# Second batch's keys and values moved into block diagonals, fourth batch's keys placed a step earlier

## The chip, the core and the metric

The kernel runs on one core of a Trainium2 chip. The core has a matrix engine (TensorE, "PE" in the profile, whose weight loads are shown apart as "PEld"), a vector engine (VectorE, "DVE"), an activation engine (ScalarE, "ACT"), a general engine (GpSimd, "POOL") and an engine that only issues transfers (SyncE, "SP"). TensorE writes its results into a small memory, PSUM; the others work on the larger SBUF, and DMA queues move data between it and the chip's main memory. The engines run beside each other, each through its own list of instructions in order, and wait for each other by semaphores. The metric is the device time of one launch, in microseconds (us); less is better.

## What is computed

Sliding-window attention over 8 batches, 8 heads, 576 positions and head size 64, followed by a two-layer network with a leaky ReLU. All inputs are float32.

```python
def _attn_ref(q, k, v):                       # each (8, 8, 576, 64)
    scale = 1.0 / np.sqrt(D)
    scores = scale * np.matmul(q, k.transpose(0, 1, 3, 2))
    mask = np.abs(pos[:, None] - pos[None, :]) <= 32
    scores = np.where(mask, scores, -1000000000.0)
    scores = scores - np.max(scores, axis=-1, keepdims=True)
    attn = np.exp(scores)
    attn = attn / (np.sum(attn, axis=-1, keepdims=True) + 1e-09)
    return np.matmul(attn, v)

x = attn_out.transpose(0, 2, 1, 3).reshape(4608, 512)
h = x @ w_in                                  # 512 x 2048
out = np.maximum(0.01 * h, h) @ w_out         # 2048 x 512
```

Each position sees only the 65 positions around it, so a block of 64 keys meets at most 128 queries.

## The kernel before

**Units of work.** Heads are taken in pairs, the two heads of a pair on partitions 0 to 63 and 64 to 127. A batch of 576 positions has two halves of 288, and an attention unit `i` is one batch, one half and one pair: `i = 8b + 4*half + pair` (`where`, L268), 64 units in all. For each unit there is a *score* (L271: keys times queries for five key blocks, into the PSUM tile `ps`, then the exponential on ScalarE and the multiplication by the window mask on VectorE or POOL), *sums* (L318: a matmul with block-diagonal ones adds up the probabilities of each query into the PSUM tile `s`, and VectorE takes the reciprocal), a *product* (L340: probabilities times values, into the PSUM tile `x`), and *scaled* (L372: VectorE multiplies product and reciprocal into `xT`, the network's input). From unit 12 on, a *join* (L310) on VectorE first adds the two layers of probabilities, so that the sums need one matmul and not two. The tiles `s` and `x` have one buffer each, and so has `ps`.

**The network.** A token group `g` is a half batch. `h_tile` (L416) makes one of 16 feature tiles for it in four matmuls of 288 columns, with the leaky ReLU on ScalarE; `o_tile` (L437) makes 128 rows of the output in 16 matmuls of 512 columns. These are the bulk of TensorE's work.

**Two forms of keys and values.** For the first two batches (`NATURAL = 2`) a head's keys lie in natural order, 64 partitions a head (`kTs`, made by transposes on TensorE and an eviction from PSUM, L203 and L212), and the values in `v0b[b]`, one tile for each of the two batches. Score and product then take, for each of five key blocks, one 64x64 matmul for each head: ten matmuls. From the third batch on, keys and values lie in block diagonals, `kbd[b % 2]` and `vbd[b % 2]`: 128x128 blocks with one head's 64x64 block in each of two quarters and zeros in the others. One 128x128 matmul serves both heads: five matmuls. The keys of these batches are cast on POOL (`cast_qk`, L227), transposed by DMA (`transpose_dma`, L238) and copied into the diagonal by two VectorE copies a pair (`place_keys`, L251), which also undo an interleaving. The values are loaded as float32 and cast by POOL into the diagonal (`cast_v`, L233).

**Order.** All engines' lists follow one written order. The first batch's attention is written out by hand (L513 to L636). Then come the first tiles of the network for the second half batch, between which the block diagonals are zeroed, `kbd` by VectorE and `vbd` by POOL (L640 to L644); POOL issues the second batch's value loads (L646, with the cast in the DMA); and SP issues the third batch's query and key loads (L648), which wait behind a tiny memset on POOL. After this the o tiles and h tiles run from a plan (L690 to L702). Each quarter of an o tile (four matmuls) and each h tile is a *turn*; `spend` (L710) runs, ahead of it, what the table `SECOND` (L667) names for the turn, which is all of the second batch's first half. From unit 12 on, `step` (L477) runs when it is due by the plan's own clock: join of unit `i + 1`, score of `i + 2`, sums, product and scaling of `i`, then `place_keys`, the casts and transposes, and the loads for the next batch. At which step the keys of a batch are placed is set in `transpose_dma`: for pair `p` of batch `b` in step `8(b - 1) + 4 + p`, and one step later for the fourth batch (`b == 3`, L247). The score that reads them first is `8b + p`, in step `8b + p - 2`.

`SECOND` before, in the turns that the change touches: scores 8 to 11 at turns 5, 6, 8 and 10; sums 8 at turn 7, sums 9 at turn 8 right behind score 10, product 8 at turn 9, sums 10 and product 9 at turn 11, sums 11 and product 10 at turn 13, score 12 at turn 14, product 11 and score 13 at turn 16. The third batch's casts and key transposes (`turned`) stand at turns 10, 12, 14 and 16. From `h_tile(2, 0)`, behind turn 16, the network reads what the second batch's units 8 to 11 have put into `xT`.

Of the kernel before, what the change touches and what calls it, by code (L numbers as in the profile page):

```python
# [9 lines left out]
FP32 = mybir.dt.float32  # L10
BF16 = mybir.dt.bfloat16
# [5 lines left out]
def kernel(  # L17
# [14 lines left out]
    nc = tc.nc  # L32

    B, H, S, D = q.shape
# [5 lines left out]
    NPAIR = H // 2  # L40
    NB = S // 64
    HALF = S // 2
# [20 lines left out]
    qf, kf, vf = {}, {}, {}  # L63
    RUN = S // 96

    NATURAL = 2
# [34 lines left out]
            in_=src[b, 2 * p:2 * (p + n)].rearrange("(p a) (i c) d -> (a i) p (c d)", a=2, c=ROW),  # L101
        )

    v0b = [const.tile([128, NPAIR, NB, D], BF16, name=f"v0b{i}") for i in range(NATURAL)]

    def load_v(b, p, engs=(nc.sync, nc.sync)):

        if engs[0] is nc.gpsimd:
            t = v0b[b][:, p]
        else:  # L110
            t = vf[b, p] = fload.tile([128, NB, D], FP32, name=f"vf{p}")
        for a in range(2):
            engs[a].dma_start(  # L113
                out=t[64 * a:64 * a + 64],
                in_=v[b, 2 * p + a].rearrange("(c p) d -> p c d", p=64),
            )

    load_v(0, 0, (nc.sync, nc.scalar))
# [4 lines left out]
    for p in range(1, NPAIR):  # L123
# [3 lines left out]
    ones_bd = const.tile([128, 128], BF16)  # L127


    kbd = [const.tile([128, NPAIR, NB, 128], BF16, name=f"kbd{i}") for i in range(2)]  # L130
    vbd = [const.tile([128, NPAIR, NB, 128], BF16, name=f"vbd{i}") for i in range(2)]
    zero = const.tile([128, 1], BF16)

    WIN = [
        [((0, 0, 48), (2, 48, 64), (4, 112, 32)), ((1, 16, 64), (3, 80, 64))],
        [((4, 0, 32), (6, 32, 64), (8, 96, 48)), ((5, 0, 64), (7, 64, 64))],
    ]

    def copy_to(eng, out, in_):
        if eng is nc.scalar:  # L140
            eng.activation(out=out, in_=in_, func=AF.Copy)
        else:
            eng.tensor_copy(out=out, in_=in_)

    HEADS = (slice(0, 64), slice(64, 128))
    GAP = 3 * 128
    wide = const.tile([128, GAP + 32 + 256], BF16)
    win = const.tile([128, 128], BF16)
# [1 line left out]
    for lo in (0, 64):  # L150
        w = win[lo:lo + 64]
        nc.gpsimd.affine_select(
            out=w, in_=w, compare_op=ALU.is_ge, fill=0.0,
# [3 lines left out]
            out=w, in_=w, compare_op=ALU.is_ge, fill=0.0,  # L157
# [30 lines left out]
    ps = scps.tile([128, 1024], FP32)  # L188
    P0 = 512 - HALF
# [9 lines left out]
    qT = {}  # L199

    trans, kTs = {}, {}

    def transpose_first(b, p, which):  # L203
# [3 lines left out]
        for c in range(ROW):  # L207
            for r in HEADS:
                nc.tensor.transpose(tp[r, c], src[r, p, c], ident[r, r])  # L209
        trans[b, p, which] = tp.rearrange("p c i -> p i c")  # L210

    def evict_first(b, p, which, eng):  # L212
        if which == "q":
            if b not in qT:
                qT[b] = attn.tile([128, NPAIR, S], BF16, name="qT")
            to = qT[b][:, p]
        else:
            to = kTs[b, p] = kt.tile([128, S], BF16, name="kT")
        copy_to(eng, to.rearrange("p (i c) -> p i c", c=ROW), trans.pop((b, p, which)))

    def value_first(b, p, eng):
        copy_to(eng, v0b[b][:, p], vf[b, p])

    def fill(eng):
        eng.memset(ps[:, 512:512 + HALF], 0.0)
# [12 lines left out]
    def transpose_dma(b, p):  # L238
        if b not in qT:
            qT[b] = attn.tile([128, NPAIR, S], BF16, name="qT")  # L240
        kT = kt.tile([128, S], BF16, name="kT")
        for t, src in ((qT[b][:, p], qb), (kT, kb)):
            nc.sync.dma_start_transpose(
                out=t.rearrange("p (c i) -> p c i", c=RUN),
                in_=src[:, p].rearrange("p c a d -> p (c a d)"),
            )
        landing.append((8 * (b - 1) + (5 if b == 3 else 4) + p, b, p, kT))  # L247

    unplaced, landing = [], []

    def place_keys():  # L251

        while landing and landing[0][0] <= state["done"]:
            unplaced.append(landing.pop(0)[1:])
        while unplaced:
            b, p, kT = unplaced.pop(0)
            for a in range(2):
                r = slice(64 * a, 64 * a + 64)
                to = kbd[b % 2][r, p, :, r]
                nc.vector.tensor_copy(  # L260
                    out=to.rearrange("p n (m c) -> p n c m", c=2),
                    in_=kT[r].rearrange("p (c n m) -> p n c m", c=2, n=NB),
                )
# [4 lines left out]
    def where(i):  # L268
        return i // 8, (i // 4) % 2, i % 4

    def score(i):  # L271
        b, hf, p = where(i)
        if b < NATURAL:
            by_n = ps[:, P0:P0 + 2 * HALF].rearrange("p (n t) -> p n t", n=2)
            for n_, blocks in enumerate(WIN[hf]):
                for blk, i0, n in blocks:
                    lo, hi = 2 * i0, 2 * (i0 + n)
                    for r in HEADS:
                        nc.tensor.matmul(  # L279
                            by_n[r, n_, lo:hi], kTs[b, p][r, 64 * blk:64 * blk + 64],  # L280
                            qT[b][r, p, hf * HALF + lo:hf * HALF + hi], start=True, stop=True,
                        )
        else:
            by_c = qT[b][:, p].rearrange("p (c i) -> p c i", c=2)
            for n_, blocks in enumerate(WIN[hf]):
                for blk, i0, n in blocks:
                    nc.tensor.matmul(  # L287
                        ps_v[:, n_, :, i0:i0 + n], kbd[b % 2][:, p, blk],
                        by_c[:, :, hf * EVEN + i0:hf * EVEN + i0 + n], start=True, stop=True,
                    )  # L290
        if b > 0:
            exps(i)
            masked(i, nc.vector if i in ON_DVE else nc.gpsimd)

    def exps(i):
        e = attn.tile([128, 2 * HALF], BF16, name="e")
        nc.scalar.activation(out=e, in_=ps[:, P0:P0 + 2 * HALF], func=AF.Exp, scale=scale)  # L297
        probs[i] = e

    def masked(i, eng):  # L300
        b, hf, p = where(i)
        e = probs[i]
        pr = prob[:, i % NPROB]
        allowed = mask_first[hf] if b < NATURAL else mask[hf].rearrange("p n c i -> p n (c i)")
        eng.tensor_mul(  # L305
            pr.rearrange("p n c i -> p n (c i)"), e.rearrange("p (n t) -> p n t", n=2), allowed,
        )
        probs[i] = [pr, None, None, None]
# [31 lines left out]
    def product(i):  # L340

        b, hf, p = where(i)
        pr = probs[i][0]
        x = xps.tile([128, HALF], FP32, name="x")
        x_v = x.rearrange("p (c i) -> p c i", c=2)
        flat = pr.rearrange("p n c i -> p n (c i)")
        parts = [(n_, *block) for n_ in range(2) for block in WIN[hf][n_]]
        if b < NATURAL:
            for n_, blk, i0, n in parts:
                lo, hi = 2 * i0, 2 * (i0 + n)  # L350
                for r in HEADS:
                    nc.tensor.matmul(  # L352
                        x[r, lo:hi], v0b[b][r, p, blk], flat[r, n_, lo:hi],
                        start=(blk == parts[0][1]), stop=(blk == parts[-1][1]),
                        skip_group_check=True,
                    )
        else:
            for n_, blk, i0, n in parts:
                nc.tensor.matmul(  # L359
                    x_v[:, :, i0:i0 + n], vbd[b % 2][:, p, blk, :], pr[:, n_, :, i0:i0 + n],  # L360
                    start=(blk == parts[0][1]), stop=(blk == parts[-1][1]),
                    skip_group_check=True,
                )
        probs[i][3] = x
# [275 lines left out]
    for f in range(4, FFC):  # L640
        h_tile(1, f)
        if f < 12:
            nc.vector.memset(kbd[f // 4 - 1][:, f % 4], 0.0)
            nc.gpsimd.memset(vbd[f // 4 - 1][:, f % 4], 0.0)  # L644
    make_mask(1, nc.gpsimd)
    for p in range(NPAIR):  # L646
        load_v(1, p, (G, G))
# [3 lines left out]
    def second_keys(p, eng):  # L651
        transpose_first(1, p, "k")
        evict_first(1, p, "k", eng)

    def second_queries(p, eng):
        transpose_first(1, p, "q")
        evict_first(1, p, "q", eng)
# [5 lines left out]
    def turned(p):  # L663
# [19 lines left out]
    }  # L683
# [14 lines left out]
    at, t = {}, 0.0  # L698
# [56 lines left out]
```

## Time and profile before

| | |
|---|---|
| median of 3 runs | 320.47 us (319.94 to 321.87) |
| the profiled execution's own time | 320.11 us |
| its span in the profile | 318.3 us |
| granted TensorE clock | 0.995 of full speed |
| busy: PE, DVE, POOL, ACT | 307.7, 213.8, 189.6, 168.3 us |
| matmuls | 2794 |
| moved by DMA | 46.11 MB, mean 145 GB/s |

The profile names each instruction by engine and by the line of the kernel (L279 is the second batch's score, L352 its product, L287 and L359 the same in block diagonals, L327 and L324 the sums, L388 the h matmuls, L446 the o matmuls, L209 the transposes, L260 the copies into the key diagonals). A line of a timeline gives start and length in us, then engine, line, operation, the tile written and the tile read, and how many such instructions were merged into the line; in square brackets stands how long the engine was idle before and whose end it waited for. Matmuls overlap, so the length of one is more than its share of TensorE's time, and what a group of them costs is read from its start to the start of the next group.

### The profile page before, as it was taken

Reading aid. Unit: us, or ns where it says so; the run is one execution under the profiler, and the core shown is the slowest. Engines: PE = TensorE matmul, PEld = TensorE weight load, DVE = VectorE, ACT = ScalarE, POOL = GpSimd, SP = SyncE. Lnnn points to the kernel's source line nnn. Section 1 sums busy time; section 2 is a strip of 40 time slices with the busy share of each in tenths; the row PEclk is TensorE's granted clock in tenths of the full one; section 3 lists DMA queues with packets and bytes.
Section 4 is the critical chain, followed back from the end, with each engine's and each line's share of the span. In section 5 each row is a group of like instructions: output and inputs, shape, how many; then the busy total and the mean of one; then the engine's idle time right before and its main releaser. Section 6 shows DMA issues by size and latency. Waiting matters only on the chain.

```text
span 318.3 us, 7099 instructions
## 1 busy us (share of the span) xinstructions
PE 307.7 (97%) x2794; PEld 202.6 (64%) x2794; DVE 213.8 (67%) x257; ACT 168.3 (53%) x370; POOL 189.6 (60%) x260
## 2 busy tenths in 40 slices
PE   5789999999999999999999999999999999999996
PEld 4557754575756747576765858576665857676653
DVE  3899528598665788688755997688745988565100
ACT  2655853472743827374652828465552837464531
POOL 8999954555466756686546866586637856330000
PEclk9799999999999999999999999999999999999999
DMA  8999999969997994599835997399933520000102
GB/s 131 143 186 207 206 172 235 154 118 223 251 218 187 205 227 110 77 222 207 187 76 124 235 200 168 74 236 168 214 75 106 107 70 35 32 37 3 66 21 80
DMA packets 107314, 46.11 MB, mean 145 GB/s; under 512 B 68752, under 2 KB 102800, under 8 KB 107280
## 3 DMA queue, kind: packets, MB, share of 16 engines
q1 hardware_dynamic: 91936, 37.91, 57.3%
q0 software_dynamic: 14752, 7.59, 18.0%
q8 instruction: 22, 0.36, 0.5%
q10 hardware_dynamic: 592, 0.15, 0.2%
q14 instruction: 12, 0.10, 0.2%
HBM read 36.70 MB, written 9.44 MB: 145 GB/s over the span
## 4 chain that ended last, share of the span: by engine, by line
PE 85%; DMA 6%; POOL 4%; DVE 3%; issue 1%; ACT 1%; DVEq 0%; ACTq 0%; POOLq 0%
PE mm L446 38%; PE mm L388 33%; DMA kb<-in_k_dram 6%; PE ps L287 4%; PE x L359 3%; POOL prob L305 2%; PE s L324 2%; DVE r L337 2%; PE tp L209 1%; PE ps L279 1%; POOL w_out_bf L509 1%; PE x L352 1%; DVE kbd L260 1%; PE s L327 1%; POOL w_in_bf L505 0%
## 5 line engine op out<-in xcount | busy, mean ns | idle before, releaser
L337 DVE RECIPROCAL r<-s 128x288 f32<-128x288 f32 x64 | 125.2, 1957 | 54.6 <-PE s L324 53.1
L388 PE MATMUL mm<-xT,w_in_bf 128*128 128x288 bf16 x1024 | 133.8, 286 | 0.3
L446 PE MATMUL mm<-w_out_bf,gT 128*128 128x512 bf16 (+2 forms) x592 | 131.5, 373 | 0.0
L399 ACT ACTIVATE gT<-mm 128x288 bf16<-128x288 f32 x256 | 101.7, 411 | 26.5 <-PE mm L388 10.0
L388 PEld LDWEIGHTS <-w_in_bf 128*128 128x128 bf16 x1024 | 98.2, 98 | 25.5 <-issue 0.6
L305 POOL TENSOR_TENSOR prob<-e,mask 128x576 bf16<-128x576 bf16 x48 | 61.2, 1274 | 81.3 <-issue 46.4
L446 PEld LDWEIGHTS <-gT 128*128 128x128 bf16 x592 | 55.6, 98 | 58.9
L451 ACT ACTIVATE o_sb<-mm 128x512 f32<-128x512 f32 (+2 forms) x37 | 21.7, 586 | 91.9 <-PE mm L446 91.9
L297 ACT ACTIVATE e<-ps 128x576 bf16<-128x576 f32 x64 | 41.4, 647 | 18.1 <-PE ps L287 8.0
L236 POOL CAST vbd<-vf 64x576 bf16<-64x576 f32 x48 | 33.2, 693 | 1.4
L374 DVE TENSOR_TENSOR xT<-x,r 128x288 bf16<-128x288 f32 x64 | 29.1, 454 | 6.2
L260 DVE COPY kbd<-kT 64x576 bf16<-64x576 bf16 x48 | 32.3, 672 | 0.3
L231 POOL CAST kb<-kf 96x384 bf16<-96x384 f32 x48 | 26.8, 583 | 1.6 <-DMA kf<-in_k_dram 1.6
L231 POOL CAST qb<-qf 96x384 bf16<-96x384 f32 x48 | 24.3, 535 | 5.4 <-DMA qf<-in_q_dram 5.3
L315 DVE TENSOR_TENSOR both<-prob 128x288 bf16<-128x288 bf16 x52 | 19.9, 382 | 4.4 <-POOL prob L305 3.6
L287 PEld LDWEIGHTS <-kbd 128*128 128x128 bf16 x240 | 15.3, 98 | 8.0 <-DVE kbd L260 1.6
L287 PE MATMUL ps<-qT,kbd 128*128 128x128 bf16 (+2 forms) x240 | 19.3, 211 | 0.6 <-DVE kbd L260 0.6
L359 PE MATMUL x<-prob,vbd 128*128 128x128 bf16 (+2 forms) x240 | 19.3, 211 | 0.0
L359 PEld LDWEIGHTS <-vbd 128*128 128x128 bf16 x240 | 15.5, 98 | 1.3
L305 POOL TENSOR_TENSOR prob<-e,wide 128x576 bf16<-128x576 bf16 x10 | 12.7, 1275 | 6.0 <-ACT e L297 6.0
L324 PE MATMUL s<-both,ones_bd 128*128 128x288 bf16 x52 | 14.9, 286 | 0.0
L113 POOL DMA_DIRECT2D v0b<-in_v_dram x14 | 10.4, 790 | 0.0
(47 smaller groups left out, 102.8 us busy)
## 6 DMA issues: line engine op xcount, KB each, us to landing
out_dram<-o_sb SPq DMA_DIRECT2D x35, 256.0 KB, 4.2
vf<-in_v_dram SPq DMA_DIRECT2D x49, 144.0 KB, 3.6
qf<-in_q_dram SPq DMA_DIRECT2D x24, 288.0 KB, 4.5
kf<-in_k_dram SPq DMA_DIRECT2D x24, 288.0 KB, 5.1
w_in_bf<-in_moe_w_in_dram POOLq DMA_DIRECT2D x4, 512.0 KB, 7.7
w_out_bf<-in_moe_w_out_dram POOLq DMA_DIRECT2D x4, 512.0 KB, 10.0
v0b<-in_v_dram POOLq DMA_DIRECT2D x14, 72.0 KB, 4.3
kb<-in_k_dram POOLq DMA_DIRECT2D x4, 144.0 KB, 4.4
```

Of the source, the lines that this page charges most:

```text
L231: nc.gpsimd.tensor_copy(out=dst[:, p, 3 * c:3 * c + 3], in_=by_c[c])
L236: nc.gpsimd.tensor_copy(out=vbd[b % 2][r, p, :, r], in_=vf[b, p][r])
L260: nc.vector.tensor_copy(out=to.rearrange("p n (m c) -> p n c m", c=2), in_=kT[r].rearrange("p (c n m) -> p n c m", c=2, n=NB),)
L287: nc.tensor.matmul(ps_v[:, n_, :, i0:i0 + n], kbd[b % 2][:, p, blk], by_c[:, :, hf * EVEN + i0:hf * EVEN + i0 + n], start=True, stop=True,)
L297: nc.scalar.activation(out=e, in_=ps[:, P0:P0 + 2 * HALF], func=AF.Exp, scale=scale)
L305: eng.tensor_mul(pr.rearrange("p n c i -> p n (c i)"), e.rearrange("p (n t) -> p n t", n=2), allowed,)
L337: nc.vector.reciprocal(r, probs[i][2])
L359: nc.tensor.matmul(x_v[:, :, i0:i0 + n], vbd[b % 2][:, p, blk, :], pr[:, n_, :, i0:i0 + n], start=(blk == parts[0][1]), stop=(blk == parts ...
L374: nc.vector.tensor_mul(place(i), x, r)
L388: nc.tensor.matmul(h[:, 0:HALF], w_in_bf[:, c, ts(f, 128)], xT[:, c, ds(g * HALF % RING, HALF)], start=(c == 0), stop=(c == DMC - 1),)
L399: nc.scalar.activation(out=to, in_=x, func=AF.Prelu, alpha=0.01)
L446: nc.tensor.matmul(o[:, lo:hi], gT[:, f, ds(128 * j % RING, 128)], w_out_bf[:, f, lo:hi], start=(f == 0), stop=(f == FFC - 1),)
```

## The change

There are four parts.

1. The second batch's scores and products take the block-diagonal form: five 128x128 matmuls in place of ten 64x64. Its keys are still transposed on TensorE and evicted in natural order; `place_keys`, called right behind the eviction, then copies them into `kbd[1]` with two VectorE copies a pair, contiguous in input and output blocks, eight copies in all. Its mask and the order of its queries stay natural.
2. Its values are cast by the DMA straight into `vbd[1]`, each head into its half of the rows, where they were cast into `v0b[1]`, which goes. `kbd[1]` and `vbd[1]` are zeroed ahead of `kbd[0]` and `vbd[0]`.
3. In `SECOND`, sums 9, 10 and 11 move a turn later: sums 9 to behind product 8, sums 10 to the turn behind product 9, sums 11 to the turn behind product 10, ahead of score 12.
4. The fourth batch's keys are placed at the same step as those of other batches, one step earlier than before.

```diff
-    v0b = [const.tile([128, NPAIR, NB, D], BF16, name=f"v0b{i}") for i in range(NATURAL)]
+    v0b = const.tile([128, NPAIR, NB, D], BF16, name="v0b")
+    kbd = [const.tile([128, NPAIR, NB, 128], BF16, name=f"kbd{i}") for i in range(2)]
+    vbd = [const.tile([128, NPAIR, NB, 128], BF16, name=f"vbd{i}") for i in range(2)]
...
     def load_v(b, p, engs=(nc.sync, nc.sync)):
-        if engs[0] is nc.gpsimd:
-            t = v0b[b][:, p]
-        else:
-            t = vf[b, p] = fload.tile([128, NB, D], FP32, name=f"vf{p}")
-        for a in range(2):
+        cast = engs[0] is nc.gpsimd
+        if not cast:
+            vf[b, p] = fload.tile([128, NB, D], FP32, name=f"vf{p}")
+        for a, r in enumerate(HEADS):
+            to = vf[b, p][r] if not cast else v0b[r, p] if b == 0 else vbd[b % 2][r, p, :, r]
             engs[a].dma_start(
-                out=t[64 * a:64 * a + 64],
-                in_=v[b, 2 * p + a].rearrange("(c p) d -> p c d", p=64),
+                out=to, in_=v[b, 2 * p + a].rearrange("(c p) d -> p c d", p=64),
             )
...
-        landing.append((8 * (b - 1) + (5 if b == 3 else 4) + p, b, p, kT))
+        landing.append((8 * (b - 1) + 4 + p, b, p, kT))
...
     def place_keys():
...
                 to = kbd[b % 2][r, p, :, r]
+                if b < NATURAL:
+                    nc.vector.tensor_copy(out=to, in_=kT[r].rearrange("p (n j) -> p n j", j=64))
+                    continue
...
     def score(i):
-        if b < NATURAL:
+        if b == 0:
...
+        elif b < NATURAL:
+            by_n = ps[:, P0:P0 + 2 * HALF].rearrange("p (n t) -> p n t", n=2)
+            for n_, blocks in enumerate(WIN[hf]):
+                for blk, i0, n in blocks:
+                    lo, hi = 2 * i0, 2 * (i0 + n)
+                    nc.tensor.matmul(
+                        by_n[:, n_, lo:hi], kbd[b % 2][:, p, blk],
+                        qT[b][:, p, hf * HALF + lo:hf * HALF + hi], start=True, stop=True,
+                    )
...
     def product(i):
-        if b < NATURAL:
+        if b == 0:
...
         else:
             for n_, blk, i0, n in parts:
+                lo, hi = 2 * i0, 2 * (i0 + n)
                 nc.tensor.matmul(
-                    x_v[:, :, i0:i0 + n], vbd[b % 2][:, p, blk, :], pr[:, n_, :, i0:i0 + n],
+                    x[:, lo:hi] if b < NATURAL else x_v[:, :, i0:i0 + n], vbd[b % 2][:, p, blk, :],
+                    flat[:, n_, lo:hi] if b < NATURAL else pr[:, n_, :, i0:i0 + n],
...
         if f < 12:
-            nc.vector.memset(kbd[f // 4 - 1][:, f % 4], 0.0)
-            nc.gpsimd.memset(vbd[f // 4 - 1][:, f % 4], 0.0)
+            nc.vector.memset(kbd[2 - f // 4][:, f % 4], 0.0)
+            nc.gpsimd.memset(vbd[2 - f // 4][:, f % 4], 0.0)
...
     def second_keys(p, eng):
         transpose_first(1, p, "k")
         evict_first(1, p, "k", eng)
+        unplaced.append((1, p, kTs[1, p]))
+        place_keys()
...
-        8: [(score, 10), (sums, 9)],
-        9: [(finish, 8)],
+        8: [(score, 10)],
+        9: [(finish, 8), (sums, 9)],
         10: [(score, 11), (turned, 0)],
-        12: [(turned, 1)],
-        11: [(sums, 10), (finish, 9)],
-        13: [(sums, 11), (finish, 10)],
-        14: [(score, 12), (turned, 2)],
+        11: [(finish, 9)],
+        12: [(sums, 10), (turned, 1)],
+        13: [(finish, 10)],
+        14: [(sums, 11), (score, 12), (turned, 2)],
```

More of the change, by code (lines that the diff above doesn't have):

```diff
@@ L102, in load_first @@
         )
-    v0b = [const.tile([128, NPAIR, NB, D], BF16, name=f"v0b{i}") for i in range(NATURAL)]
+    v0b = const.tile([128, NPAIR, NB, D], BF16, name="v0b")
+    kbd = [const.tile([128, NPAIR, NB, 128], BF16, name=f"kbd{i}") for i in range(2)]
+    vbd = [const.tile([128, NPAIR, NB, 128], BF16, name=f"vbd{i}") for i in range(2)]
+    HEADS = (slice(0, 64), slice(64, 128))
     def load_v(b, p, engs=(nc.sync, nc.sync)):
-        if engs[0] is nc.gpsimd:
-            t = v0b[b][:, p]
-        else:
-            t = vf[b, p] = fload.tile([128, NB, D], FP32, name=f"vf{p}")
-        for a in range(2):
+        cast = engs[0] is nc.gpsimd
[3 more added lines that the diff above has]
+            to = vf[b, p][r] if not cast else v0b[r, p] if b == 0 else vbd[b % 2][r, p, :, r]
             engs[a].dma_start(
-                out=t[64 * a:64 * a + 64],
-                in_=v[b, 2 * p + a].rearrange("(c p) d -> p c d", p=64),
+                out=to, in_=v[b, 2 * p + a].rearrange("(c p) d -> p c d", p=64),
             )
@@ L127 @@
     ones_bd = const.tile([128, 128], BF16)
-    kbd = [const.tile([128, NPAIR, NB, 128], BF16, name=f"kbd{i}") for i in range(2)]
-    vbd = [const.tile([128, NPAIR, NB, 128], BF16, name=f"vbd{i}") for i in range(2)]
     zero = const.tile([128, 1], BF16)
@@ L143, in copy_to @@
             eng.tensor_copy(out=out, in_=in_)
-    HEADS = (slice(0, 64), slice(64, 128))
     GAP = 3 * 128
@@ L221, in value_first @@
     def value_first(b, p, eng):
-        copy_to(eng, v0b[b][:, p], vf[b, p])
+        copy_to(eng, v0b[:, p], vf[b, p])
     def fill(eng):
@@ L352, in product @@
                     nc.tensor.matmul(
-                        x[r, lo:hi], v0b[b][r, p, blk], flat[r, n_, lo:hi],
+                        x[r, lo:hi], v0b[r, p, blk], flat[r, n_, lo:hi],
                         start=(blk == parts[0][1]), stop=(blk == parts[-1][1]),
```

## The prediction

> **What bounds the kernel now.** I read the page's engine rows first, then the busy time by stretch.
>
> ```profile
> span 318.3 us, 7099 instructions
> PE 307.7 (97%) x2794; PEld 202.6 (64%) x2794; DVE 213.8 (67%) x257; ACT 168.3 (53%) x370; POOL 189.6 (60%) x260
> ```
> ```profile
> 39.65:124.00 84.35, 83.39 (x805) 51.35 (x800) 59.47 (x72) 43.63 (x92) 48.86 (x69) 1.00 1.04 195
> 124.00:300.00 176.00, 176.00 (x1396) 117.91 (x1395) 126.23 (x147) 96.01 (x217) 102.83 (x135) 1.00 0.60 125
> ```
> In the second fence the columns are the stretch, its length, then busy time and instructions of PE, PEld, DVE, ACT and POOL, the granted clock, the DMA share and GB/s. From 39.65 us on TensorE is the bound: 83.39 of 84.35 us, then 176.00 of 176.00. So time taken from TensorE's list of work behind 39.65 comes off the end, unless something else becomes late. But 97% busy hides what a matmul costs, since matmuls overlap. I therefore measure in start to start, from TensorE's timeline.
>
> **The cost of a group.** One score, or one product with the values, is ten 64x64 matmuls in the second batch and five 128x128 matmuls from the third batch on. Here are both forms between the same neighbours (start, length, engine, line, operation):
>
> ```profile
> 60.35 0.43 PE L352 MATMUL x<-prob,v0b 64*64 64x96 bf16 x10
> 60.62 0.41 PE L279 MATMUL ps<-qT,kT 64*64 64x64 bf16 x10
> 60.96 1.04 PE L446 MATMUL mm<-w_out_bf,gT 128*128 128x512 bf16 x4
> 61.83 1.63 PE L388 MATMUL mm<-xT,w_in_bf 128*128 128x288 bf16 x12
> 63.39 0.43 PE L279 MATMUL ps<-qT,kT 64*64 64x64 bf16 x10
> 63.76 0.30 PE L324 MATMUL s<-both,ones_bd 128*128 128x288 bf16 x1
> 63.98 0.43 PE L352 MATMUL x<-prob,v0b 64*64 64x64 bf16 x10
> 64.34 3.11 PE L388 MATMUL mm<-xT,w_in_bf 128*128 128x288 bf16 x24
> ...
> 80.34 1.14 PE L388 MATMUL mm<-xT,w_in_bf 128*128 128x288 bf16 x8
> 81.32 0.40 PE L287 MATMUL ps<-qT,kbd 128*128 128x96 bf16 x5
> 81.56 0.29 PE L324 MATMUL s<-both,ones_bd 128*128 128x288 bf16 x1
> 81.68 0.40 PE L359 MATMUL x<-prob,vbd 128*128 128x96 bf16 x5
> 81.92 4.57 PE L388 MATMUL mm<-xT,w_in_bf 128*128 128x288 bf16 x36
> ```
> Pace first: eight h matmuls take 81.32 - 80.34 = 0.98 us, 0.1225 each; four o matmuls 61.83 - 60.96 = 0.87, 0.217 each. The twelve h matmuls from 61.83 thus fill up to 63.30, and the next h matmul starts at 64.34: score, sums and product cost 1.04 us. In the block-diagonal form they cost 81.92 - 81.32 = 0.60, of which 0.24 a group. The saving is 0.44 for two groups, **0.22 a group**. The ten small matmuls alone need only 0.27 (60.35 to 60.62, where a second small group follows). So 0.03 is in the matmuls and nearly 0.2 in going into the 64x64 form and out of it.
>
> The Trainium skill, TensorEngine Tiling (Array Packing), section Key Properties, says that a change of tiling mode, unlike a change of tile, drains the array; the gaps around the small groups agree with it, about 0.1 us at each end. The page TensorE: Matmul & The Clock Gate, section Measured speedup vs the span model, adds about 4 ns for each packed tile, so packing as such should lose nothing. By it alone sixteen groups would give next to nothing (a rival below).
>
> **The sum on TensorE.** Sixteen groups change (scores 8 to 15, products 8 to 15):
> - Scores 8 and 9 stand directly ahead of transposes, which stay 64x64; the switch is only moved. Worth 0.03 each, counted as nothing.
> - Product 11 and score 13 share their switches: from 60.35 less the gap of 0.10, to 60.96, is 0.71 against 0.48 after: 0.23 for both.
> - The other twelve: 12 x 0.22 = 2.64.
>
> Together **2.87 us**.
>
> **The moved sums.** The sums share one PSUM buffer, which the reciprocal of the sums before must give back:
>
> ```profile
> 49.35 0.43 PE L279 MATMUL ps<-qT,kT 64*64 64x96 bf16 x10
> 50.10 0.41 PE L327 MATMUL s<-prob,ones_bd 128*128 128x288 bf16 x2 [0.32 <-DVE r L337]
> ...
> 54.56 1.90 PE L446 MATMUL mm<-w_out_bf,gT 128*128 128x512 bf16 x8
> 56.50 0.41 PE L327 MATMUL s<-prob,ones_bd 128*128 128x288 bf16 x2
> ...
> L337 DVE RECIPROCAL r<-s 128x288 f32<-128x288 f32 x64 | 125.2, 1957 | 54.6 <-PE s L324 53.1
> L374 DVE TENSOR_TENSOR xT<-x,r 128x288 bf16<-128x288 f32 x64 | 29.1, 454 | 6.2
> ```
> A score ahead of sums takes 0.37 (63.39 to 63.76), so sums 9 could have come at 49.72 and came at 50.10: 0.38 lost. Sums 11 could have come at 54.56 + 8 x 0.217 = 56.29 and came at 56.50: 0.21 lost. After the change sums 9 stand a turn later, behind product 8, at about 50.5, and the reciprocal of sums 8 ends near 50.0: no wait. But with TensorE now some 1.5 us ahead, VectorE is next in line. From 48.0 on it has three reciprocals of 1.96, two masks of 0.46 (row below) and two scalings of 0.45, 7.7 us, and about 0.7 of handovers and of waiting for exps 10 and sums 10; so the reciprocal of sums 10 ends at about 56.4, while sums 11 would be reached at 56.1. I leave 0.3 lost there: **0.29 saved** of 0.59.
>
> **The eight copies added.** The second batch's keys now pass through VectorE into the block diagonals, two copies of 64x576 for each pair. The trace has no such contiguous copy:
>
> ```profile
> 39.48 0.65 ACT L141 ACTIVATE kT<-tp 128x576 bf16<-128x576 bf16 x1 [0.31 <-PE tp L209]
> L260 DVE COPY kbd<-kT x48: 498/690/828, 66.7 to 262.8; 64x576 bf16<-64x576 bf16 x48
> L305 DVE TENSOR_TENSOR prob<-e,wide 128x576 bf16<-128x576 bf16 x6 | 3.0, 492 | 5.4 <-ACT e L297 4.7 <-POOL qb L231 0.6
> 45.79 0.46 DVE L305 TENSOR_TENSOR prob<-e,wide 128x576 bf16<-128x576 bf16 x1 [2.75 <-ACT e L297]
> ```
> The upper bound is the interleaving copy at its slowest, 0.83 us; from below nothing excludes less than the mask of the same 576 contiguous elements, 0.46, so I keep 0.2 as an end. I take 0.46, since it is the contiguous one: 3.7 us of VectorE. What hides them is idle time: VectorE waited 2.75 us ahead of the mask at 45.79, and more ahead of that. Pair 0's copies follow ScalarE's eviction (39.48 + 0.65) and are done at about 41.1, and score 8 needs them at 44.4. Pair 1's eviction on VectorE queues behind them (to 41.9; copies to 42.8, needed at 46.1). At 0.83 the copies hold up mask 9 and so the reciprocal of sums 8 by some 1.3 us, and sums 9 then wait 0.9 us.
>
> **The fourth batch's keys one step earlier.**
>
> ```profile
> 114.64 3.62 PE L446 MATMUL mm<-w_out_bf,gT 128*128 128x512 bf16 x16
> 118.64 0.41 PE L287 MATMUL ps<-qT,kbd 128*128 128x96 bf16 x5 [0.38 <-DVE kbd L260]
> ...
> 119.25 3.59 PE L388 MATMUL mm<-xT,w_in_bf 128*128 128x288 bf16 x28
> 123.06 0.41 PE L287 MATMUL ps<-qT,kbd 128*128 128x96 bf16 x5 [0.22 <-DVE kbd L260]
> ```
> The score at 118.64 was possible at 114.64 + 16 x 0.217 = 118.10, that at 123.06 at 119.25 + 28 x 0.1225 = 122.68: 0.54 + 0.38 = **0.92 us** lost, because the copies stand directly ahead of the score that reads them. One step earlier they are done some 4 us before it. What could be late next is the transposed key itself:
>
> ```profile
> 102.47 1.82 SPq L243 DMA_TRANSPOSE kT<-kb  x1
> ...
> 107.97 1.44 DVE L260 COPY kbd<-kT 64x576 bf16<-64x576 bf16 x2
> DMA to landing us min/median/max: 2.5/3.2/5.9
> ```
> Pair 1's transpose is issued at 102.47, the tightest of the four; its copy would now be asked for at about 108.0, in the place where pair 0's copy stands. That leaves 5.5 us against a median landing of 3.2 and a longest of 5.9. So I expect no wait, at worst 0.4 on VectorE; behind it stand the next join and reciprocal, and TensorE asks for these a step of 4 us later.
>
> **What moves besides.** The transposes of the third batch's keys no longer wait for the second batch's scores to free their buffers; SP is earlier with them and with the value loads behind them, worth nothing by itself. The zeroing only swaps order. The values' loads stay eight, with the same runs read:
>
> ```profile
> 38.53 5.92 POOL L113 DMA_DIRECT2D v0b<-in_v_dram  x8
> 49.74 0.95 POOL L231 CAST qb<-qf 96x384 bf16<-96x384 f32 x2 [5.26 <-DMA qf<-in_q_dram]
> 54.33 1.06 POOL L231 CAST kb<-kf 96x384 bf16<-96x384 f32 x2
> 59.37 1.27 POOL L305 TENSOR_TENSOR prob<-e,wide 128x576 bf16<-128x576 bf16 x1 [3.98 <-ACT e L297]
> ...
> v0b<-in_v_dram POOLq DMA_DIRECT2D x14, 72.0 KB, 4.3
> kb<-in_k_dram POOLq DMA_DIRECT2D x2, 288.0 KB, 13.4
> ```
> The first values land near 39.3 + 4.3 = 43.6, and product 8 reads them at about 50.3.
>
> **Sum:** 2.87 + 0.29 + 0.92 = 4.08 us. The profiled execution took 320.11, 0.36 under the median of 320.47; 320.11 - 4.08 = 316.03, and on the median's footing **316.4 us**. With all waits gone it is 0.3 less, and faster copies add nothing.
>
> **The rivals.**
> - *VectorE takes over* (chance 0.17). With copies of 0.83 sums 9 wait 0.9 us and sums 11 0.3, so the moved sums lose 0.6 instead of gaining 0.29. For: VectorE is busy 59.47 of 84.35 us here and the turns get shorter. Against: its idle time ahead of 45.79. Time 317.3.
> - *The fourth batch's wait returns* (0.10), as a copy that waits for its transpose and holds the reciprocals behind it: 0.92 is not gained, 317.3. Against: the batches from the fifth on have this spacing, and there TensorE is busy for 176.00 of 176.00.
> - *The small groups give nothing* (0.08): if the gaps come from the neighbours and not from the form, the body's 16 x 0.03 = 0.5 remains: 320.47 - 0.5 - 0.29 - 0.92 = 318.8. Against it stand the two rows of groups above, with the same neighbours.
> - *Slower* (0.10): the value loads into half rows hold back the query and key loads of the third batch, which SP issues only when POOL has issued the values. The casts they feed stand on POOL ahead of mask 12: they ended at 55.4, and mask 12 would now be wanted at 57.8. Beyond 2.4 us of delay mask 12, join 12 and the scaling of 11 behind it are late, one for one, and the first h tile waits. From 6.5 us it is slower than before. If landings of 4.3 us became 13.4, as the first key loads of this batch show, 9.1 - 2.4 = 6.7 is lost: 320.47 - 4.08 + 6.7 = 323.1. Against: the run read and the bytes of each load don't change.
>
> The Trainium skill, SBUF — State Buffer, section SBUF: two separate sides, tells of a "DVE blocks DMA" trap: a VectorE copy between SBUF tiles in its two-port mode keeps GpSimd from writing DMA descriptors. By it the copies up to 44.45, some six of them, would delay POOL's loads by up to 6 x 0.46 = 2.8 us, an estimate, of which 0.4 would be felt. The trace of before shows only the reverse, a mask on VectorE held 0.6 us by a cast on POOL.
>
> **How the numbers follow.** The forecast has 0.55, the rivals 0.17, 0.10, 0.08 and 0.10. About 1%, 3.2 us, is what a measurement here tells from no change. Faster by more than that means under 317.3: the forecast and some of the first two rivals, 0.62. Slower by more than 1% is the upper half of the last rival, 0.06. The rest is 0.32. The range goes from 315.5 (all waits gone, and 0.6 for spread) to 318.7, past the first two rivals, and leaves out the third and the last.
>
> **What would show it.** Right: the second batch's scores and products as five 128x128 matmuls, 0.24 us start to start; 0.60 for a step's three groups at score 14; no wait of scores on the block-diagonal copies near 115 to 120; the first h tile of the second batch starting 1.8 us earlier, at about 60.0, and the third batch's first product 3.1 us earlier. Wrong: a wait of the second batch's sums on the reciprocal of over 1 us, copies over 0.8 us, POOL's casts of the third batch starting later than 52, or gaps on TensorE behind 124.

## The result, and the profile after

The changed kernel takes 319.05 us (median of 20 runs, 318.02 to 320.00) against 320.56 for the kernel before: a ratio of 0.9944 with an interval of 0.9929 to 0.9960. It is faster, by 1.8 us by the ratio, where 4.1 was forecast. Ten of its twenty executions had a mean granted clock of 0.999 or 1.000 and took 318.02 to 319.00 us, and the ten with 0.984 to 0.995 took 319.10 to 320.00, so a median of few executions moves by up to a microsecond with how many of each it holds.

The profiled execution took 319.33 us. Before it is compared, one thing has to be taken out of it. Two rows each of before and of after follow, before first: the stretch from 16 to 24 us (the granted TensorE clock is the third number from the end) and TensorE's first key transposes of the second batch.

```profile
16.00:24.00 8.00, 6.91 (x95) 4.67 (x96) 7.67 (x8) 4.31 (x10) 7.92 (x9) 1.00 1.16 187
38.97 0.75 PE L209 MATMUL tp<-ident,kb 64*64 64x64 bf16 x36 [0.25 <-DMA kb<-in_k_dram]
```
```profile
16.00:24.00 8.00, 6.85 (x85) 4.50 (x86) 6.41 (x7) 3.31 (x7) 6.74 (x8) 0.79 1.13 181
40.27 0.75 PE L208 MATMUL tp<-ident,kb 64*64 64x64 bf16 x36
```
In this execution the clock was at 0.79 in this stretch of the first batch, which the change doesn't touch, and the transposes came 1.3 us later. I therefore count from them: the *rest* of the span took 318.3 - 38.97 = 279.33 us before and 317.6 - 40.27 = 277.33 after, 2.0 less. Now TensorE's timeline after:

```profile
61.21 1.63 PE L401 MATMUL mm<-xT,w_in_bf 128*128 128x288 bf16 x12
62.68 0.40 PE L290 MATMUL ps<-qT,kbd 128*128 128x64 bf16 x5
62.92 0.29 PE L335 MATMUL s<-both,ones_bd 128*128 128x288 bf16 x1
63.05 0.40 PE L371 MATMUL x<-prob,vbd 128*128 128x64 bf16 x5
63.28 3.10 PE L401 MATMUL mm<-xT,w_in_bf 128*128 128x288 bf16 x24
...
70.25 0.40 PE L298 MATMUL ps<-qT,kbd 128*128 128x96 bf16 x5
70.82 0.28 PE L335 MATMUL s<-both,ones_bd 128*128 128x288 bf16 x1 [0.16 <-DVE r L348]
71.38 0.41 PE L371 MATMUL x<-prob,vbd 128*128 128x64 bf16 x5 [0.28 <-DVE xT L387]
71.63 3.62 PE L459 MATMUL mm<-w_out_bf,gT 128*128 128x512 bf16 x16
75.09 0.40 PE L298 MATMUL ps<-qT,kbd 128*128 128x96 bf16 x5
75.70 0.28 PE L335 MATMUL s<-both,ones_bd 128*128 128x288 bf16 x1 [0.21 <-DVE r L348]
76.27 0.41 PE L371 MATMUL x<-prob,vbd 128*128 128x64 bf16 x5 [0.28 <-DVE xT L387]
76.52 3.62 PE L459 MATMUL mm<-w_out_bf,gT 128*128 128x512 bf16 x16
79.97 0.90 PE L401 MATMUL mm<-xT,w_in_bf 128*128 128x288 bf16 x6
81.31 0.41 PE L401 MATMUL mm<-xT,w_in_bf 128*128 128x288 bf16 x2 [0.43 <-DVE xT L387]
81.55 0.40 PE L298 MATMUL ps<-qT,kbd 128*128 128x96 bf16 x5
```
The gain, counted from the transposes, stands like this along the way:
- First h tile of the second batch: 61.83 - 38.97 = 22.86 before, 61.21 - 40.27 = 20.94 after: 1.92 gained.
- Score 14, sums and product: 63.28 - 62.68 = 0.60 us, where it was 1.04.
- Score 16, step 14: 71.78 - 38.97 = 32.81 before (row below), 70.25 - 40.27 = 29.98 after: 2.83 gained.
- Step 14 itself: 71.63 - 70.25 = 1.38 where the same three groups can take 0.60: 0.78 lost. Step 15: 76.52 - 75.09 = 1.43: 0.83 lost. Then six h matmuls, which fill 0.735, and the seventh comes at 81.31 and not 80.70: 0.60 lost. Together **2.2 us**.
- Score 18: 81.32 - 38.97 = 42.35 before, 81.55 - 40.27 = 41.28 after: 1.07 gained.

```profile
71.78 0.40 PE L287 MATMUL ps<-qT,kbd 128*128 128x96 bf16 x5
```

The gain was made and then most of it was given back in three places within 11 us, each time in a wait on VectorE (on a reciprocal, on a scaling). The fourth batch's part came as forecast: its score at 118.32 follows its sixteen o matmuls (114.87 + 16 x 0.217 = 118.34) without a wait, and so does the next, after 28 h matmuls (118.92 + 28 x 0.1225 = 122.35).

```profile
114.87 3.62 PE L459 MATMUL mm<-w_out_bf,gT 128*128 128x512 bf16 x16
118.32 0.40 PE L298 MATMUL ps<-qT,kbd 128*128 128x96 bf16 x5
...
122.35 0.40 PE L298 MATMUL ps<-qT,kbd 128*128 128x96 bf16 x5
```
Why was VectorE late? Here are its work in steps 12 to 15 and POOL's masks of the same time, after:

```profile
63.51 0.58 DVE L326 TENSOR_TENSOR both<-prob 128x288 bf16<-128x288 bf16 x1 [2.17 <-POOL prob L316]
64.01 1.95 DVE L348 RECIPROCAL r<-s 128x288 f32<-128x288 f32 x1
...
67.53 1.37 DVE L326 TENSOR_TENSOR both<-prob 128x288 bf16<-128x288 bf16 x1
68.82 1.95 DVE L348 RECIPROCAL r<-s 128x288 f32<-128x288 f32 x1
71.24 1.91 DVE L262 COPY kbd<-kT 64x576 bf16<-64x576 bf16 x2
76.13 2.08 DVE L262 COPY kbd<-kT 64x576 bf16<-64x576 bf16 x2
...
67.45 1.28 POOL L316 TENSOR_TENSOR prob<-e,wide 128x576 bf16<-128x576 bf16 x1 [0.86 <-ACT e L308]
71.48 1.30 POOL L316 TENSOR_TENSOR prob<-e,mask 128x576 bf16<-128x576 bf16 x1 [2.75 <-ACT e L308]
76.56 1.27 POOL L316 TENSOR_TENSOR prob<-e,mask 128x576 bf16<-128x576 bf16 x1 [2.22 <-issue]
```
Three VectorE operations have grown: join 14 takes 1.37 us, the copies of pairs 1 and 2 take 1.91 and 2.08 a pair. Each lies over a POOL mask and ends just behind it: the mask at 67.45 ends at 68.73, the join at 68.90; the mask at 71.48 ends at 72.78, the copies at 73.15; the mask at 76.56 ends at 77.83, the copies at 78.21. Joins 15 and 16, behind these copies at 73.19 and 78.24, took 0.59 and not 0.31, and lay beside POOL's casts of values (from 72.74 and 77.78). In the kernel before, the same copies stood at 70.52 and 74.78, took 1.03 and 1.33, and missed the masks at 68.65, 73.01 and 77.53:

```profile
70.52 1.03 DVE L260 COPY kbd<-kT 64x576 bf16<-64x576 bf16 x2
74.78 1.33 DVE L260 COPY kbd<-kT 64x576 bf16<-64x576 bf16 x2
...
68.65 1.28 POOL L305 TENSOR_TENSOR prob<-e,wide 128x576 bf16<-128x576 bf16 x1 [1.77 <-ACT e L297]
73.01 1.28 POOL L305 TENSOR_TENSOR prob<-e,mask 128x576 bf16<-128x576 bf16 x1 [3.08 <-ACT e L297]
77.53 1.28 POOL L305 TENSOR_TENSOR prob<-e,mask 128x576 bf16<-128x576 bf16 x1 [1.79 <-issue]
```
My theory from this: TensorE and with it the masks have moved ahead (counted from the transposes, masks 15 and 16 stand 2.5 and 2.8 us earlier than before), VectorE has not to the same degree (reciprocal 12 stands 1.6 us earlier), since join 13 waits 2.17 us for mask 13 and holds reciprocal 12 behind it (it starts at 64.01, its sums began at 62.92). From there VectorE's work falls under POOL's masks and is held until they end. The rivals: VectorE's load as such is the bound; the fourth batch's earlier placing has moved trouble forward; or the loss is in the front of the kernel.

### The profile page after: what moved, and what is told of

Read it like the earlier page. It is cut to its first block, busy times and chain, and to the rows that moved or that the text cites. A ratio compares the mean times of both kernels' runs of the same rounds, so it can differ in the third digit from the quotient of the medians.

```text
span 317.6 us, 6957 instructions
## 1 busy us (share of the span) xinstructions
PE 306.0 (96%) x2714; PEld 203.9 (64%) x2714; DVE 219.6 (69%) x265; ACT 167.9 (53%) x370; POOL 190.5 (60%) x260
## 4 chain that ended last, share of the span: by engine, by line
PE 75%; POOL 10%; DVE 7%; DMA 4%; issue 2%; ACT 1%; SPq 0%; DVEq 0%; ACTq 0%; POOLq 0%
PE mm L459 33%; PE mm L401 33%; PE x L371 4%; DVE r L348 4%; PE ps L298 3%; POOL vbd L657 2%; DMA qf<-in_q_dram 2%; PE s L335 2%; POOL vbd L116 2%; DMA qb<-in_q_dram 2%; POOL prob L316 2%; DVE kbd L262 2%; DVE both L326 1%; POOL kb L99 1%; POOL qb L99 1%
## 5 line engine op out<-in xcount | busy, mean ns | idle before, releaser
L262 DVE COPY kbd<-kT 64x576 bf16<-64x576 bf16 x48 | 33.2, 692 | 0.3
L326 DVE TENSOR_TENSOR both<-prob 128x288 bf16<-128x288 bf16 x52 | 21.5, 413 | 3.2 <-POOL prob L316 2.5
L371 PE MATMUL x<-prob,vbd 128*128 128x96 bf16 (+1 forms) x280 | 22.5, 211 | 0.6 <-DVE xT L387 0.6
L371 PEld LDWEIGHTS <-vbd 128*128 128x128 bf16 x280 | 17.8, 98 | 4.1 <-DVE xT L387 1.7
L657 POOL MEMSET vbd<- 128x1152 bf16 x8 | 8.1, 1097 | 0.0
```

Source lines behind the costliest of these rows:

```text
L262: nc.vector.tensor_copy(out=to.rearrange("p n (m c) -> p n c m", c=2), in_=kT[r].rearrange("p (c n m) -> p n c m", c=2, n=NB),)
L371: nc.tensor.matmul(x[:, lo:hi] if b < NATURAL else x_v[:, :, i0:i0 + n], vbd[b % 2][:, p, blk, :], flat[:, n_, lo:hi] if b < NATURAL else ...
```

## The experiments

Each was timed beside the kernel before on the same chip. Times are medians, ratios are against the kernel before, with their intervals. Beside them stands the rest of the one profiled execution, from the first key transposes to the end, where the granted clock was 1.00 in every run: 279.33 us before and 277.33 in the changed kernel.

**The fourth batch's part alone, and all but it.**

```diff
-        landing.append((8 * (b - 1) + (5 if b == 3 else 4) + p, b, p, kT))
+        landing.append((8 * (b - 1) + 4 + p, b, p, kT))
```


> The kernel before with the fourth batch's keys placed a step earlier and nothing else. By the prediction's step the waits of 0.54 and 0.38 us near 118 and 123 us go: 320.56 - 0.92 = 319.6 us, and no wait of a score on the copies. If the transposes land too late for it, VectorE waits for them and the time stays at 320.5.

> The changed kernel with the fourth batch's keys placed where they were before. If that part is worth 0.92 us whatever stands ahead of it: 319.05 + 0.92 = 320.0 us, which leaves 0.6 us to all the rest of the change. If the loss of the changed kernel comes from this part, it is faster than 319.05.

Alone: 319.41 us, ratio 0.9962 (0.9944 to 0.9981), about 1.2 us less. All but it: 319.36 us, ratio 0.9971 (0.9953 to 0.9989), about 0.9 less. The 0.92 of the prediction lies inside the first interval. The two add up to 2.1, near the 1.8 of the whole change, so the fourth batch's part neither causes the loss nor hides it. By the rest it saves 1.05 us alone (278.28 for 279.33) and 0.92 on top of the others (277.33 for 278.25). The median of all but it lies under the 320.0 that I expected. The other parts, priced at 3.16, are worth some 0.9 by the ratio and 1.08 by the rest. The front of the kernel is not where the gain is lost: in this run, with a clock of 1.00 up to there, the first key transposes came at 39.15, for 38.97 before, and the first h tile 20.95 us behind them, for 20.94 in the changed kernel.

**Without three of POOL's masks**, in the changed kernel.

```diff
+    UNMASKED = (15, 16, 17)
...
     def exps(i):
+        if i in UNMASKED:
+            pr = prob[:, i % NPROB]
+            nc.scalar.activation(out=pr.rearrange("p n c i -> p (n c i)"),
+                                 in_=ps[:, P0:P0 + 2 * HALF], func=AF.Exp, scale=scale)
+            probs[i] = [pr, None, None, None]
+            return
```


> The changed kernel without the window mask of units 15, 16 and 17: their exponentials go straight into the probability tile, so POOL has no mask to do there and that part of the computation is left out. Theory of the shared resource: the copies of the third batch's keys and the joins on VectorE are stretched because POOL's masks 15 to 17 run at the same time. Then the pairs of copies go from 1.91 and 2.08 us back to 1.03 to 1.33, join 14 from 1.37 to 0.31, and TensorE's waits in steps 14 to 16 shrink from 2.2 to under 0.8: about 317.5. If VectorE is late for its order alone, the copies get short but the waits stay: 318.5 or more. If the loss is in the front: 319.0.

Measured: 316.25 us, ratio 0.9864 (0.9840 to 0.9887). VectorE and TensorE there:

```profile
63.79 0.58 DVE L336 TENSOR_TENSOR both<-prob 128x288 bf16<-128x288 bf16 x1 [2.17 <-POOL prob L326]
64.29 1.95 DVE L358 RECIPROCAL r<-s 128x288 f32<-128x288 f32 x1
67.80 0.31 DVE L336 TENSOR_TENSOR both<-prob 128x288 bf16<-128x288 bf16 x1
70.46 1.29 DVE L262 COPY kbd<-kT 64x576 bf16<-64x576 bf16 x2
74.72 1.04 DVE L262 COPY kbd<-kT 64x576 bf16<-64x576 bf16 x2
```
```profile
70.54 0.40 PE L299 MATMUL ps<-qT,kbd 128*128 128x96 bf16 x5
...
71.14 3.62 PE L469 MATMUL mm<-w_out_bf,gT 128*128 128x512 bf16 x16
```
Join 13 is as late as in the changed kernel (it waits the same 2.17 us) and reciprocal 12 stands as far behind it. But join 14 is back at 0.31, the copies at 1.29 and 1.04, and step 14 costs 0.60. All the waits of steps 14 to 16 are gone, more than I expected (317.5 us, waits under 0.8). The rest is 275.15, 2.18 less than with the masks, which is the 2.2 that was lost. So the stretched operations make the waits, and the masks make most of the stretching (where 1.29 remains, POOL ran casts of values). That the joins need not wait for masks here is not the reason: in the changed kernel no join from 14 on waits for POOL. The lateness of reciprocal 12 alone would have cost nothing.

**The same masks left out of the kernel before**, as a control.

> The kernel before without the window mask of units 15, 16 and 17, which is left out of the computation. It had no wait of TensorE in steps 12 to 16, so by the theory nothing is to be had: 320.3 to 320.6. If leaving the masks out saves time by itself, the 2.8 us that it saved in the changed kernel show here too: 317.7.

Measured: 320.20 us, ratio 0.9990 (0.9972 to 1.0009). Leaving the masks out is worth nothing by itself: the rest is 279.21, 0.12 less than with them. Between the two kernels without the masks the rest differs by 4.06 us, where the prediction had 4.08.

**Without the third batch's copies**, in the changed kernel.

```diff
             b, p, kT = unplaced.pop(0)
+            if b == 2:
+                continue
```


> The changed kernel without the copies of the third batch's keys into the block diagonal (eight copies on VectorE in steps 12 to 15); its scores are then made from zeros, so that part of the computation is left out. Theory: with 1.05 to 2.08 us less a step VectorE catches up at once, join 14 no longer falls on a mask, and the 2.2 us of waits in steps 14 to 16 go: 316.3 to 316.9. If something else than VectorE's lateness makes the waits, they stay: 319.

Measured: 316.64 us, ratio 0.9874 (0.9844 to 0.9904), no wait of TensorE in steps 12 to 16, and a rest of 275.12, 2.21 less. With the run without masks this says that neither VectorE's copies nor POOL's masks are too much alone: it is the two at once.

**The third batch's casts earlier on POOL.**

```diff
-        13: [(finish, 10)],
-        14: [(sums, 11), (score, 12), (turned, 2)],
-        16: [(join, 12), (finish, 11), (score, 13), (turned, 3)]
+        13: [(finish, 10), (turned, 2)],
+        14: [(sums, 11), (turned, 3), (score, 12)],
+        16: [(join, 12), (finish, 11), (score, 13)]
```


> The changed kernel with the third batch's casts and transposes of pairs 2 and 3 moved ahead on POOL, to turns 13 and 14, in front of mask 12. Theory: VectorE falls behind in step 12, since join 13 stands ahead of reciprocal 12 and waits for mask 13, which stands behind the casts on POOL; TensorE then waits 2.2 us in steps 14 to 16. With the casts out of the way reciprocal 12 starts with its sums, about 1 us earlier, and most of the 2.2 us come back: 317.0 to 317.7. Rival: the gain is lost in the front, where the first key transposes came at 40.27 and not 38.97 us: no change, 319.0.

Measured: 317.39 us, ratio 0.9904 (0.9879 to 0.9929). The median is inside what the theory gave, but partly by luck: the rest is 277.00, only 0.33 less than in the changed kernel. The trace shows a price that I had not named:

```profile
64.06 0.90 PE L401 MATMUL mm<-xT,w_in_bf 128*128 128x288 bf16 x6 [1.73 <-DVE xT L387]
62.28 1.37 DVE L326 TENSOR_TENSOR both<-prob 128x288 bf16<-128x288 bf16 x1 [1.98 <-POOL prob L316]
60.98 2.50 POOL L316 TENSOR_TENSOR prob<-e,wide 128x576 bf16<-128x576 bf16 x2
71.52 1.03 DVE L262 COPY kbd<-kT 64x576 bf16<-64x576 bf16 x2
75.37 1.33 DVE L262 COPY kbd<-kT 64x576 bf16<-64x576 bf16 x2
```
The copies are short again and the waits of steps 14 to 16 are gone. In their place masks 12 and 13 come late on POOL, join 12 waits for the first and is stretched by the second (1.37 us), scaling 11 stands behind it, and the first h tile waits 1.73 us. So the 2.2 us came back, as the theory says, and most of them were lost again further ahead.

**The join behind the scaling**, in the changed kernel.

```diff
-        if JOINED - 1 <= i < NC - 1:
-            join(i + 1)
         if i < NC - 2:
             score(i + 2)
         weighted(i)
+        if JOINED - 1 <= i < NC - 1:
+            join(i + 1)
```


> The changed kernel with each step's join behind its scaling instead of ahead of its reciprocal. Theory: VectorE's copies and joins of steps 13 to 15 fall on POOL's masks because join 13 holds reciprocal 12 some 1 us behind its sums. With the join behind, reciprocal 12 starts within 0.4 us of its sums, the two copies of pairs 1 and 2 take 1.03 to 1.33 us again, and TensorE's waits in steps 14 to 16 go from 2.2 to under 0.5 us: 316.9 to 317.4, if the later joins don't come late for their sums. If VectorE's load as such is the bound there, the waits stay: 319.

Measured: 316.91 us, ratio 0.9882 (0.9854 to 0.9910), with the whole output computed: faster than both kernels. The rest is 275.37, 1.96 less than in the changed kernel.

```profile
64.21 1.96 DVE L348 RECIPROCAL r<-s 128x288 f32<-128x288 f32 x1 [1.92 <-PE s L335]
71.27 1.03 DVE L262 COPY kbd<-kT 64x576 bf16<-64x576 bf16 x2
75.39 1.04 DVE L262 COPY kbd<-kT 64x576 bf16<-64x576 bf16 x2
```
Reciprocal 12 now waits for its own sums alone (they began at 63.88 in this run), the copies take 1.03 and 1.04, and no wait on VectorE is left in steps 14 to 16. In step 13 the sums come 0.26 us late (67.69 behind a score at 67.19), since join 13 now lies partly under mask 14 and takes 0.99.

**The same order in the kernel before.**

> The kernel before with each step's join behind its scaling. If the new order is worth something only where TensorE has run ahead of VectorE (theory), only the two waits of the fourth batch, 0.92 us, can change: 319.6 to 320.6. If the order is simply better by itself, the gain is that of the changed kernel, 2 us: 318.5.

Measured: 322.11 us, ratio 1.0051 (1.0033 to 1.0070): slower, which I had not expected. The waits of TensorE name the reason (us in total, times, longest; the kernel before stands first).

```profile
PE ps L287 <- DVE kbd L260: 0.6, 2, 0.4
```
```profile
PE ps L287 <- DVE kbd L260: 1.6, 3, 0.6
```
With the join ahead of them, the copies of the fourth batch, which stood directly ahead of the scores that read them, are later still: TensorE's own waits for them go from 0.6 to 1.6 us. From start to start these scores come 2.3 us late in sum, where it was 0.92. The order that saves 2 us in the changed kernel costs 1.6 here by the ratio, and 1.2 by the rest (280.56). That it would pay with the fourth batch's keys placed a step earlier, or only where TensorE has run ahead, no run shows, since these were not tried one by one.

**The moved sums.** First in the changed kernel, then with the join behind the scaling:

```diff
-        8: [(score, 10)],
-        9: [(finish, 8), (sums, 9)],
-        11: [(finish, 9)],
-        12: [(sums, 10), (turned, 1)],
-        13: [(finish, 10)],
-        14: [(sums, 11), (score, 12), (turned, 2)],
+        8: [(score, 10), (sums, 9)],
+        9: [(finish, 8)],
+        11: [(sums, 10), (finish, 9)],
+        12: [(turned, 1)],
+        13: [(sums, 11), (finish, 10)],
+        14: [(score, 12), (turned, 2)],
```


> The changed kernel with sums 9, 10 and 11 in their old turns. The prediction gave the moved sums 0.29 us; without them sums 9 wait for reciprocal 8 again (over 0.4 us) and sums 11 for reciprocal 10. If TensorE's lead only ends in the later wait on VectorE, time lost here is no time lost: 319.0. If it counts in full: 319.3 to 319.6.

> The changed kernel with the join behind the scaling and with sums 9, 10 and 11 in their old turns: what the moved sums are worth where no later wait takes the lead away. The prediction gave 0.29 us: 316.91 + 0.3 = 317.2; with the waits of the trace of before in full, 317.5. If the moved sums are worth nothing: 316.9.

Measured: 319.26 us, ratio 0.9958 (0.9941 to 0.9976), and 317.33, ratio 0.9898 (0.9874 to 0.9923). In the changed kernel the old turns cost 0.2 us by the medians and 0.4 by the ratios, without the later waits 0.4 and 0.5. The intervals overlap in both, so the times alone suggest the order and don't show it. By the rest the old turns cost 0.70 us (278.03 for 277.33) and 0.93 (276.30 for 275.37), in one profiled execution each. In the first of these runs the first h tile already stands 61.89 - 40.27 = 21.62 us behind the transposes, for 20.94, and sums 9 wait 0.44 us for reciprocal 8. So the time lost in the turns does count, although later waits follow, and the moved sums are worth more than the 0.29 predicted.

**The changed kernel once more.**

> The changed kernel itself, beside the three that follow. Expected 318.9 to 319.2 us, with the 2.2 us of waits in steps 14 to 16 in its trace as before; they follow from the order of the work and not from one execution.

Measured: 318.24 us, ratio 0.9926 (0.9901 to 0.9951), under the 318.9 that I expected at least. The rest is the same, 277.32 for 277.33. The waits are the same in place and length: 0.6 us of products and 0.4 of sums and of an h matmul on VectorE, and the three stretched places in TensorE's timeline.

## Why the prediction was wrong

The time came out at 319.05, past the upper end of 318.7, since 2.2 us of the 4.08 were given back. Of the signs of being right, the third batch's first product failed: it came 1.07 us earlier (81.68 - 38.97 before, 81.91 - 40.27 after), and not 3.1. Point by point:

- **The cost of a group: right.** Score 14, sums and product cost 0.60 us, as read from the third batch, and the second batch's first h tile came 1.92 us earlier, for the 1.8 forecast for groups and moved sums together. The rival by which small groups give nothing falls.
- **The eight copies: right.** They took 0.447 us each (0.46 taken), in VectorE's idle time; neither scores 8 and 9 nor sums 9 waited for them.
- **The moved sums: right in kind, too small in size.** 0.70 and 0.93 us by the rest, 0.4 to 0.5 by the ratios, for 0.29. With the old turns, part of what the groups save is lost again in longer waits on the reciprocals, so how the gain divides between groups and sums depends on which is taken first. That the two together came out so near the forecast is in part luck.
- **The fourth batch's keys: right.** 0.92 forecast, 0.9 read from the trace (2.01 us of lead at the score at 122.35, for 1.07 at score 18), 1.2 by the ratio of that part alone, 1.05 and 0.92 by the rest with and without it.
- **The value loads: right.** POOL issued them in 5.91 us for 5.92, and POOL's first cast of the third batch came at 50.04 for 49.74. The slower rival had nothing to act on. The Trainium skill's "DVE blocks DMA" trap (SBUF — State Buffer, section SBUF: two separate sides) gave up to 2.8 us here by my estimate; the trace doesn't agree, as far as it goes: of the eight copies, which ran from 41.46 to 48.54, four (the rows below) fell into the loads' issue, from 39.79 to 45.70, and it was no longer than without them:

```profile
39.79 5.91 POOL L116 DMA_DIRECT2D vbd<-in_v_dram  x8
41.46 0.91 DVE L260 COPY kbd<-kT 64x576 bf16<-64x576 bf16 x2 [3.29 <-ACT kT L141]
43.19 0.91 DVE L260 COPY kbd<-kT 64x576 bf16<-64x576 bf16 x2
```
- **The step that failed** is the first one, in its last clause: time taken from TensorE "comes off the end, unless something else becomes late". I looked for what becomes late only beside the parts of the change, in the turns 5 to 16 and at the fourth batch. *VectorE takes over* was a rival, but in the wrong place and for the wrong reason: in the turns, from slow added copies. It took over in steps 13 to 15, where the change adds nothing to VectorE, because its unchanged joins and copies met POOL's masks. I carried their durations over from the profile of before (0.31 us, 1.03 to 1.33 a pair), as if an operation had a length of its own. The runs showed 1.37, 1.91 and 2.08 us under the masks, and from them 2.2 us of waits on TensorE that the sum had put at nothing. The rows of before held only for its own order in time. The trace of before had a warning in it, and I misread it: the mask on VectorE that I called held 0.6 us by a cast on POOL was waiting for its exponential, which ScalarE ran from 53.09 to 53.74, and began 0.11 us behind its end, as the mask at 50.57 began 0.10 behind its own (50.47). What the cast at 53.32 goes with is the mask's length, 0.73 us for 0.46 elsewhere.

```profile
53.85 0.73 DVE L305 TENSOR_TENSOR prob<-e,wide 128x576 bf16<-128x576 bf16 x1 [0.64 <-POOL qb L231]
```

The section of the Trainium skill named above also says that VectorE, in a two-port mode or with two SBUF inputs (then only against a GpSimd operation that reads SBUF), and GpSimd share a pair of SBUF ports, held for a whole instruction, while the other engine waits in full. There the trace agrees: each of the three stretched operations ends 0.2 to 0.4 us behind the mask that it lay under. In which mode the copies ran, no run shows. Had I laid that rule over the masks, I would have had a reason to look for the overlap.

## What to carry to other kernels

When one engine gets faster, the others' work doesn't stay where the old profile shows it: lay the new order of time over every pair of engines that can hold each other, also where the change touches neither of them. An operation's length in a profile holds for its neighbours of that moment; ask for its shortest and its longest, and what ran beside the longest. And a join or a scaling that waits for a third engine should not stand ahead of the operation that frees a single PSUM buffer; but where it goes instead depends on what is late there, and the same move cost 1.2 to 1.6 us in the kernel before.

## What the runs showed of the hardware

- VectorE's copies and two-input additions between SBUF tiles are held by a two-input multiplication on GpSimd that reads and writes SBUF: an addition of 0.31 us took 1.37, a pair of copies of 1.03 took up to 2.08, and each ended 0.2 to 0.4 us behind the end of GpSimd's operation. Taking the three multiplications away gave back 2.2 us of the changed kernel's rest and 0.1 of the other's. Beside GpSimd's casts, which have one input, the stretching was smaller: 0.59 for 0.31, and 1.55 for 1.03 a pair (at 79.06 in the kernel before). A VectorE reciprocal, which reads PSUM, was not stretched: 1.96 us at 72.34 in the kernel before, over the whole mask at 73.01. What it is that the two engines share, no run here shows.
- Going from 128x128 matmuls to a group of 64x64 ones and back costs about 0.2 us of TensorE's time (0.46 us a group between large matmuls, 0.27 where another small group follows), six times what the small matmuls themselves cost over the large ones (0.27 to 0.24 us).
- A contiguous VectorE copy of 64x576 bf16 elements takes 0.447 us, into blocks of 64 with a stride of 128; the interleaving copy of the same size took 0.50 to 0.83 in the kernel before.
